# Attention backward: dK and dV by 64-row matmuls with two heads side by side, and a new order of the program

**Chip, cores, metric.** One Trainium2 chip, one core. The metric is the device time of one execution in microseconds (us), the median of several. Ratios and intervals use fast runs alone: the mean time of one kernel's fast runs over that of the other's of the same rounds, so a ratio is not quite that of the medians that are quoted. The span of a profile is some 1.8 us shorter than the time of the same execution (735.8 and 737.6 us before).

**Names.** PE multiplies matrices and writes to the memory PSUM; DVE and ACT copy from there and do the vector work; POOL does small work and the small DMA transfers; SP issues the large transfers.

## The reference

Forward and backward of grouped-query attention, all in bf16: 32 batches, 4 key heads, 32 query heads with 4 queries each (so 32 query rows per key head, 128 in all), 2048 keys, 128 dimensions.

```python
def _fwd_reference(q, k, v):
    ...                                   # k, v repeated 8 times over the heads
    scores = jnp.einsum("bhqd,bhkd->bhqk", q, k) * scale
    p = _softmax(scores, axis=-1)
    return jnp.einsum("bhqk,bhkd->bhqd", p, v)

def reference(q, k, v, grad_out):
    _out, _vjp = jax.vjp(_f, q, k, v)
    _grads = _vjp(grad_out)
    return (_out, *_grads)                # out, dq, dk, dv
```

K, V, dK and dV are 67 MB each and everything else is small, so some 275 MB pass through DMA in any case.

## The kernel before

The program is fully unrolled. Each piece of work ("unit") of a batch has a place in one global order; each engine executes its units in that order. The places, and for every copy out of PSUM whether DVE or ACT does it, stand in long tables that came out of a search. Units of neighbouring batches are interleaved. A batch has these on PE: transposes of K and V (`KT`, `VT`, 16 units of 8 matmuls), transposes `ET`, `DT` (two units each), and scores `S`, `DP`, outputs `O`, `DQ`, and `DV`, `DK` (four units each, of 512 keys). In the cuts below, comments and `...` are mine.

```python
BLOCK, TRIG, FIRST, FETCH, BACK = 256, 216, 446, 3.4, 0.33    # planner: PE's program blocks
...                                                            # tables PLACE, ENGINE, SHIFT, SWAP
        elif name == "dop":
            t["dop"] = sm_pool.tile([P, D], BF16, name="dop_sb")
            nc.gpsimd.tensor_scalar(out=t["dop"][:], in0=t["go"][:], scalar1=t["rinv"][:], scalar2=None, op0=ALU.mult)
...
        elif name in ("DV", "DK"):
            ...
            lhs, rhs = ("e", "dop") if name == "DV" else ("ds", "qp")
            for j in range(CPQ):                      # 4 blocks of 128 keys
                c = CPQ * i + j
                for h in range(NH):                   # 4 heads, one row tile of 32 each
                    r = slice(32 * h, 32 * h + 32)
                    w = QW * (h % 2) + P * j
                    nc.tensor.matmul(accs[h // 2][:, w:w + P], lhsT=t[lhs][r, P * c:P * c + P],
                                     rhs=t[rhs][r, :], start=True, stop=True, tile_position=(32 * h, 0))
...
        elif name in ("Os", "DQs"):                   # stores of O and dQ, on POOL's queue
            nc.gpsimd.dma_start(...)
...
    with tc.manual_schedule():
        for u in order:
            emit(u)
```

A matmul is two PE instructions, a weight load and the matmul itself (14,400 of each on the page of this kernel). A batch has 900 PE instructions.

## Time and profile before

| | before |
|---|---|
| time, median of 4 | 736.72 us (734.19 to 740.49) |
| PE busy, instructions | 613.7 us, 28,800 |
| DVE, ACT busy | 581.7 us each |
| DMA | 274.74 MB, mean 373 GB/s |
| mean granted PE clock | 0.982 |

Matmuls overlap in PE's pipeline (in this trace a narrow one takes 214 ns in the median, and 16 of them follow each other in 0.33 us), so "busy" is the time in which at least one is in it. A wait marked "issue" has no releaser in the profile: no semaphore, no other engine. The lines themselves are in the prediction.

### The profile page before, as it was taken

How to read it: one execution, taken by the hardware profiler on the slowest of the kernel's cores; microseconds unless marked ns; L12 is line 12 of the kernel's file. 1: busy time of each engine (PE TensorE's matmuls, PEld its weight loads, DVE VectorE, ACT ScalarE, POOL GpSimd, SP SyncE). 2: the span in 40 equal slices, each digit the busy share in tenths (PEclk: the TensorE clock that was granted, in tenths of full speed). 3: DMA queues.
4: the chain of work that ended last, by engine and by line, in shares of the span. 5: the costliest groups of instructions: out<-in, count | busy, mean ns of one | idle time of the engine just before them, and what ended most of it. 6: DMA issues, size and time to landing. Idle time of an engine off the chain costs nothing.

```text
span 735.8 us, 32599 instructions
## 1 busy us (share of the span) xinstructions
PE 613.7 (83%) x14400; PEld 458.3 (62%) x14400; DVE 581.7 (79%) x835; ACT 581.7 (79%) x862; POOL 112.0 (15%) x230
## 2 busy tenths in 40 slices
PE   6798887988878988888888898887988878898885
PEld 5576665665655765656666666665766656676563
DVE  3788887878877887877878788887878878888874
ACT  4788886878877887877877688886888878887884
POOL 3121110111101111111111111110111111110110
PEclk9999999999999999999999999999999999999998
DMA  9999999999999999999999989999999999989957
GB/s 346 408 401 407 378 411 355 392 383 346 401 356 390 370 400 365 390 400 342 389 355 395 396 331 402 377 402 404 348 402 366 401 383 386 372 314 389 378 222 283
DMA packets 75917, 274.74 MB, mean 373 GB/s; under 512 B 8192, under 2 KB 8192, under 8 KB 75776
## 3 DMA queue, kind: packets, MB, share of 16 engines
q1 hardware_dynamic: 71680, 268.46, 94.7%
q0 software_dynamic: 4096, 4.20, 1.7%
q8 instruction: 112, 1.84, 0.9%
q14 instruction: 29, 0.24, 0.1%
HBM read 136.31 MB, written 136.31 MB: 371 GB/s over the span
## 4 chain that ended last, share of the span: by engine, by line
PE 66%; issue 10%; ACT 9%; DMA 8%; DVE 6%; SPq 0%; DVEq 0%; POOLq 0%; ACTq 0%; POOL 0%
PE psum L426 31%; PE psum L488 10%; PE psum L525 9%; PE psum L437 9%; PE psum L477 7%; ACT dk_sb L530 4%; DMA v_sb<-in_v_dram 4%; DVE ds_sb L510 4%; DMA k_sb<-in_k_dram 3%; ACT dt_sb L394 2%; ACT e_sb L453 2%; DMA out_dram<-dv_sb 1%; DVE dv_sb L530 1%; DVE mjunk L444 1%; ACT vt_sb L394 1%
## 5 line engine op out<-in xcount | busy, mean ns | idle before, releaser
L426 PE MATMUL psum<-ident,v_sb 128*128 128x128 bf16 x2048 | 159.9, 222 | 38.3 <-DVE ds_sb L510 13.1
L426 PEld LDWEIGHTS <-v_sb 128*128 128x128 bf16 x2048 | 122.5, 99 | 89.5 <-issue 68.0
L530 ACT CAST dv_sb<-psum 128x1024 bf16<-128x1024 f32 x158 | 155.8, 1025 | 12.4 <-PE psum L525 9.0
L530 ACT CAST dk_sb<-psum 128x1024 bf16<-128x1024 f32 x161 | 157.8, 1025 | 9.6 <-PE psum L525 9.3
L426 PE MATMUL psum<-ident,k_sb 128*128 128x128 bf16 x2048 | 149.5, 222 | 6.7 <-DMA k_sb<-in_k_dram 4.6
L530 DVE CAST dk_sb<-psum 128x1024 bf16<-128x1024 f32 x95 | 113.6, 1221 | 32.1 <-PE psum L525 29.0
L426 PEld LDWEIGHTS <-k_sb 128*128 128x128 bf16 x2048 | 119.5, 99 | 26.5 <-issue 8.9
L530 DVE CAST dv_sb<-psum 128x1024 bf16<-128x1024 f32 x98 | 119.4, 1220 | 17.9 <-PE psum L525 17.7
L397 DVE COPY vt_sb<-psum 128x1024 bf16<-128x1024 bf16 x128 | 87.3, 684 | 36.5 <-PE psum L426 25.7
L394 ACT COPY vt_sb<-psum 128x512 f32<-128x512 f32 x128 | 77.8, 610 | 40.4 <-PE psum L426 40.2
L397 DVE COPY kt_sb<-psum 128x1024 bf16<-128x1024 bf16 x126 | 84.2, 683 | 19.9 <-PE psum L426 17.3
L394 ACT COPY kt_sb<-psum 128x512 f32<-128x512 f32 x130 | 74.7, 615 | 22.9 <-PE psum L426 22.0
L525 PE MATMUL psum<-qp_sb,ds_sb 32*128 32x128 bf16 x2048 | 62.0, 218 | 29.3 <-ACT et_sb L394 9.4
L510 DVE SCALAR_TENSOR_TENSOR ds_sb<-psum,delta,e_sb 128x1024 bf16<-128x1024 f32 x64 | 81.8, 1278 | 1.0 <-PE psum L437 1.0
L453 ACT ACTIVATE e_sb<-psum,m 128x1024 bf16<-128x1024 f32 x64 | 70.8, 1112 | 6.3 <-DVE mjunk L444 4.7
L525 PEld LDWEIGHTS <-ds_sb 32*128 32x128 bf16 x2048 | 34.6, 93 | 49.8 <-issue 36.1
L525 PE MATMUL psum<-dop_sb,e_sb 32*128 32x128 bf16 x2048 | 60.5, 217 | 4.9 <-issue 2.2
L488 PE MATMUL psum<-k_sb,dt_sb 128*32 128x128 bf16 x2048 | 49.1, 224 | 12.5 <-issue 12.3
L499 POOL DMA_DIRECT2D out_dram<-dq_sb x32 | 17.8, 557 | 265.4 <-ACT dq_sb L495 250.5
L477 PE MATMUL psum<-ident,e_sb 128*128 128x128 bf16 x512 | 38.8, 219 | 16.2 <-ACT dk_sb L530 14.1
L462 POOL TENSOR_SCALAR dop_sb<-go_sb,rinv 128x128 bf16<-128x128 bf16 x32 | 19.7, 616 | 211.8 <-DVE rinv L459 209.3
L525 PEld LDWEIGHTS <-e_sb 32*128 32x128 bf16 x2048 | 35.8, 92 | 22.9 <-issue 8.8
(44 smaller groups left out, 643.2 us busy)
## 6 DMA issues: line engine op xcount, KB each, us to landing
k_sb<-in_k_dram SPq DMA_DIRECT2D x128, 512.0 KB, 8.9
v_sb<-in_v_dram SPq DMA_DIRECT2D x128, 512.0 KB, 8.8
out_dram<-dv_sb SPq DMA_DIRECT2D x64, 1024.0 KB, 8.0
out_dram<-dk_sb SPq DMA_DIRECT2D x64, 1024.0 KB, 7.7
q_sb<-in_q_dram POOLq DMA_DIRECT2D x32, 32.0 KB, 5.4
go_sb<-in_grad_out_dram POOLq DMA_DIRECT2D x32, 32.0 KB, 5.7
out_dram<-o_sb POOLq DMA_DIRECT2D x32, 32.0 KB, 5.1
out_dram<-dq_sb POOLq DMA_DIRECT2D x32, 32.0 KB, 6.1
```

Source lines behind the costliest of these rows:

```text
L394: nc.scalar.copy(out=out.rearrange("p c d -> p (c d)").bitcast(FP32), in_=in_.rearrange("p c d -> p (c d)").bitcast(FP32))
L397: nc.vector.tensor_copy(out=out, in_=in_)
L426: nc.tensor.transpose(out=ps[:, j, :], in_=t[x, h][:, 8 * i + j, :], identity=ident[:])
L437: nc.tensor.matmul(t[name, i][r, QW * w:QW * w + QW], lhsT=t["qdt"][:, side, r], rhs=t[x, h, i][:, CPQ * w:CPQ * w + CPQ, :], start=True, ...
L453: nc.scalar.activation(out=t["e"][:, 2 * QW * i:2 * QW * i + 2 * QW], in_=t["S", i][:], func=ACT.Exp, bias=t["m"][:], scale=scale, accum_o ...
L462: nc.gpsimd.tensor_scalar(out=t["dop"][:], in0=t["go"][:], scalar1=t["rinv"][:], scalar2=None, op0=ALU.mult)
L477: nc.tensor.transpose(out=ps[:, j, :], in_=src[:, P * c:P * c + P], identity=ident[:])
L488: nc.tensor.matmul(t[name][r, 0:D], lhsT=t[xt, c // 8][:, c % 8, r], rhs=t[x, h][:, c, :], start=(c == 0), stop=(c == C - 1), tile_positio ...
L499: nc.gpsimd.dma_start(out=(o_r if name == "Os" else dq_r)[b], in_=t["o" if name == "Os" else "dq"][:])
L510: nc.vector.scalar_tensor_tensor(out=t["ds"][:, w], in0=t["DP", i][:], scalar=t["dl"][:], in1=t["e"][:, w], op0=ALU.subtract, op1=ALU.mult)
L525: nc.tensor.matmul(accs[h // 2][:, w:w + P], lhsT=t[lhs][r, P * c:P * c + P], rhs=t[rhs][r, :], start=True, stop=True, tile_position=(32 * ...
L530: copy(out=t[name[:2], "out", g][:, :, CPQ * i:CPQ * i + CPQ, :].rearrange("p h c d -> p h (c d)"), in_=t[name[:2], i][g][:].rearrange("p ...
```

## The change

Intent: fewer PE instructions, so that PE waits less for its own program. Two heads share one matmul of 64 rows; the moving operand has 256 columns, of which one half is zero in the rows of each head, so the heads' results come out side by side. POOL makes the two masked halves. Along with it all tables were made anew, with the wide form's costs in the planner, the planner's model of block fetches was changed, and stores of O and dQ moved to some four batches later.

```diff
-BLOCK, TRIG, FIRST, FETCH, BACK = 256, 216, 446, 3.4, 0.33
+BLOCK, TRIG, FIRST, FETCH, BACK = 256, 216, 446, 3.15, 0.33
...                                        (PLACE, SHIFT, SWAP: all numbers new)
-    QTe="D", KTe="DADADAAD", VTe="ADDADAAD", ETe="AA", DTe="AA", Oe="D", DQe="A", DVe="AADAADAD", DKe="ADAAADAD")
+    QTe="A", KTe="DADAAAAA", VTe="ADDADAAD", ETe="AA", DTe="AD", Oe="D", DQe="A", DVe="AADAADAD", DKe="DAAAADAD")
...
+            if b == 2:
+                nc.gpsimd.memset(evenodd[:], 0.0)
...                                        (1 or scale where row's head is even / odd)
-            t["dop"] = sm_pool.tile([P, D], BF16, name="dop_sb")
-            nc.gpsimd.tensor_scalar(out=t["dop"][:], in0=t["go"][:], scalar1=t["rinv"][:], scalar2=None, op0=ALU.mult)
+            t["dop"] = dop_bd[b % CAP["dop"]]
+            for k in range(2):
+                nc.gpsimd.tensor_scalar(out=t["dop"][:, k, :], in0=t["go"][:], scalar1=t["rinv"][:],
+                                        scalar2=evenodd[:, k:k + 1], op0=ALU.mult, op1=ALU.mult)
...                                        (qp the same)
-                for h in range(NH):
-                    r = slice(32 * h, 32 * h + 32)
-                    w = QW * (h % 2) + P * j
-                    nc.tensor.matmul(accs[h // 2][:, w:w + P], lhsT=t[lhs][r, P * c:P * c + P],
-                                     rhs=t[rhs][r, :], start=True, stop=True, tile_position=(32 * h, 0))
+                for g in range(2):
+                    r = slice(64 * g, 64 * g + 64)
+                    nc.tensor.matmul(accs[g][:, 2 * P * j:2 * P * j + 2 * P], lhsT=t[lhs][r, P * c:P * c + P],
+                                     rhs=t[rhs][r, :, :].rearrange("p h d -> p (h d)"), start=True, stop=True,
+                                     tile_position=(64 * g, 0))
...                                        (the copies out of PSUM read the new layout)
```

## The prediction

> **What bounds the kernel now.** I read the busy row first, then the slices, the queues and the chain, then single batches. The page says that no compute engine is full, and that the DMA engines nearly are:
>
> ```profile
> PE 613.7 (83%) x14400; PEld 458.3 (62%) x14400; DVE 581.7 (79%) x835; ACT 581.7 (79%) x862; POOL 112.0 (15%) x230
> ...
> DMA  9999999999999999999999989999999999989957
> ...
> q8 instruction: 112, 1.84, 0.9%
> ...
> PE 66%; issue 10%; ACT 9%; DMA 8%; DVE 6%; SPq 0%; DVEq 0%; POOLq 0%; ACTq 0%; POOL 0%
> ```
>
> The row of DMA digits tempts one to stop: the engines are busy, so the change can win nothing. But the kernel moves 274.74 MB at a mean of 373 GB/s, and single stretches reach over 400, so some of the time is lost. The chain is mostly PE, with 10% "issue": time in which an engine waited for nothing that the profile shows. The q8 line says what this may be: 112 packets of 16 KB, that is one per 256 of the 28,800 PE instructions. PE's program itself comes in by DMA.
>
> I then cut the middle into batches (the 32 reciprocals on DVE mark them) and asked for busy time, granted clock and GB/s of each:
>
> ```profile
> 398.80:423.20 24.40, 20.24 (x454) 14.82 (x453) 18.17 (x27) 18.28 (x27) 3.48 (x7) 0.93 1.02 400
> 423.20:444.10 20.90, 18.47 (x452) 14.04 (x450) 18.01 (x26) 18.16 (x27) 3.48 (x7) 1.00 0.91 339
> 444.10:467.00 22.90, 18.74 (x453) 14.12 (x450) 18.02 (x26) 18.28 (x27) 3.48 (x7) 1.00 1.02 404
> 467.00:488.00 21.00, 18.57 (x453) 13.96 (x450) 18.02 (x26) 18.16 (x27) 3.48 (x7) 1.00 0.99 375
> 488.00:512.20 24.20, 20.23 (x457) 14.96 (x458) 18.16 (x27) 18.27 (x27) 3.48 (x7) 0.93 1.03 406
> 512.20:533.30 21.10, 18.83 (x463) 14.18 (x466) 17.97 (x26) 18.06 (x27) 3.48 (x7) 1.00 0.96 356
> ```
>
> After the span come PE, weight loads, DVE, ACT, POOL, clock, DMA share, GB/s. The same work takes about 21 us in every second batch and 23 to 24.4 in the others. The long ones have the clock at 0.93; the lack of data shows in the batch after (339, 356 GB/s), since a late batch makes its stores late. The PE timeline of a long one shows the cause:
>
> ```profile
> 412.90 0.34 PE L525 MATMUL psum<-qp_sb,ds_sb 32*128 32x128 bf16 x9
> 415.22 0.40 PE L525 MATMUL psum<-qp_sb,ds_sb 32*128 32x128 bf16 x7 [1.98 <-issue]
> 415.55 1.03 PE L426 MATMUL psum<-ident,v_sb 128*128 128x128 bf16 x8
> ```
>
> PE stops inside a group of 16 matmuls that has all its inputs, for 1.98 us, and the transposes after it take 1.03 us in place of 0.62. I numbered PE's instructions in the order of the trace: of all gaps over 0.3 us, 42.9 us stand before one single position of 256 (number 193 modulo 256), no other has over 7.6. At several of those gaps the 16 KB packet lands just as PE resumes. So these are waits for the program. A long batch loses 1.98 us standing and about 1.7 us at half clock (0.07 x 24.4), which is the 3.5 us by which it is longer. My reading: DMA supply and PE limit together, and what spoils PE's part is instruction fetch.
>
> [...] the trace has eight transposes 0.55 us apart, 8 x 56 ns and some 0.1 us for the mode change. [...] the trace has 0.93 in batches with a long stop and 1.00 in the others. [...] 16 matmuls of 128 columns follow each other in 0.33 us, that is 4 x 56 ns plus 0.1.
>
> **The change, part by part.** (1) dV and dK are made with 64-row tiles: two heads share a matmul, and its 256 moving columns hold the rows of one head beside those of the other, with zeros where they don't belong. Per 512-key group that is 8 matmuls of 256 columns in place of 16 of 128, two at once in place of four. *Cost:* 4 x 109 + 110 = 545 ns a group in place of 334 (the timeline's spacing), so 0.21 us more; there are 8 groups in a batch and 256 in all: 54 us of PE time. Summing the spacings of all groups, PE needs 566 us before (17.7 a batch) and 620 after (19.4).
>
> (2) *Gain:* PE instructions fall from 900 to 772 a batch, 28,800 to 24,704, so 96 blocks in place of 112. More than the number counts where they lie. [...] In the old order a run dV, O, O, O, O, dV is 192 instructions in about 2 us[...]. So nearly all of the 42 us should go, and with it the half clock behind the long stops. Also 772 is 3 x 256 + 4: the boundaries fall at nearly the same places in each batch. I leave 5 us of stops.
>
> (3) POOL makes two masked copies of dO' and Q' in place of one each: 64 more operations of 0.37 to 0.62 us (the rows of its two), about 30 us on an engine that is 15% busy. In front of the first dV of a batch this adds up to 0.6 us.
>
> (4) The order is new: stores of O and dQ are issued some four batches later, so POOL no longer blocks on them; about two K copies a batch go from DVE to ACT and one dS-transposed copy the other way. With 613 ns on ACT and 684 on DVE each this is around +20 us ACT and -25 DVE, both still near 80%. PSUM copies read in pieces of 128 rather than 512 elements; I count no cost for that.
>
> *Sum.* The first reciprocal starts at 17.5 us, the last at 711.8, 31 periods of 22.4 on average, and 24 us follow. Without fetch stops a period is what the undisturbed batches show, 20.9 to 21.1. That cannot hold for all: 8.59 MB a batch at the 400 to 409 GB/s of full stretches is 21.2 us. I add 0.3 us because PE now fills 19.4 of it and has less room for its other waits: 21.5. The tail is bound by PE and copies, so it gets 8 x 0.21 = 1.7 us longer. 17.5 + 31 x 21.5 + 25.7 = 709.7; I say 709.
>
> **The rivals.** *PE becomes the bound.* The undisturbed batches have 21.0 - 17.7 = 3.3 us of other PE waits. If all of these are needed, a period is 19.4 + 3.3 = 22.7, and the time 747. For it: PE at 66% of the chain. Against: in those batches PE also waits for loads, and the DMA queue has its own limit of 21.2, so part of the 3.3 us is slack. Half of it real gives 21.2 anyway. *The transfers hide it all.* If the DMA rate of 373 GB/s is the memory's own and the stops only move waiting about, the time stays at 725 to 737. For it: nines everywhere. Against: 339 and 356 GB/s beside 404 in neighbouring batches. *POOL in the way.* If the second masked copy delays each dV, 31 x 0.6 = 19 us come back: 728. Against: POOL sat idle 209 us waiting for the reciprocal, and other PE work stands between softmax and the first dV in the order.
>
> **Range and chances.** The DMA floor is 274.74 MB at 405 GB/s, 678 us, plus some 3 us at the head and 16 at the tail where little moves: 697, which is why I go no lower than 698. A period of 22.0 (half the rivals' losses) gives 725, the upper end at 727. "Faster by over 2%" starts at 722, a mean period of 21.9. I give that 0.75, within 2% 0.23 (mostly rival one and three), slower 0.02.
>
> **What would show it.** Right: PE busy up by 30 to 60 us and 12,352 matmuls; q8 with about 96 packets; "issue" waits of PE down by 40 us or more; the granted clock near 1.00 in the middle; batches of even length at 21.2 to 21.8 us; GB/s near 400 in most slices. Wrong: batches even but at 22.5 with PE waiting for ACT or DVE (rival one); fetch stops still there, at a new fixed place of each batch; waits of PE for the masked copies (rival three); the dV and dK groups at other than 0.55 us.

## The result, and the profile after

708.88 us (707.75 to 711.37, 10 runs) against 736.34 (16 runs); ratio 0.9624, 95% interval 0.960 to 0.9647: faster by 3.8%.

In all that follows, a "stop" is the time from the start of one PE instruction to that of the next, where it is over 0.3 us and stands before position 193 modulo 256. It includes what the earlier instruction still runs: of the 42.9 us before, some 34 are idle time, of the 6.1 us after some 4.4.

The page of the changed kernel, in the same rows as in the prediction, with two rows of the costliest groups added:

```profile
PE 634.1 (90%) x12352; PEld 471.4 (67%) x12352; DVE 559.6 (79%) x779; ACT 606.4 (86%) x918; POOL 134.1 (19%) x303
...
DMA  8999999999999999999999999999999999999967
...
q8 instruction: 96, 1.57, 0.8%
...
PE 52%; DMA 25%; ACT 10%; DVE 7%; issue 4%; POOL 0%; DVEq 0%; POOLq 0%; ACTq 0%
...
L472 POOL TENSOR_SCALAR dop_sb<-go_sb,rinv,evenodd 128x128 bf16<-128x128 bf16 x64 | 27.9, 439 | 532.7 <-DVE rinv L468 507.7
...
L536 PE MATMUL psum<-dop_sb,e_sb 64*128 64x256 bf16 x1024 | 87.1, 271 | 1.9 <-DVE et_sb L400 0.5
```

"issue" fell from 10% to 4% of the chain, and DMA rose from 8% to 25%: the end is now set by transfers to a good part. The stops are 6.1 us, against 42.9. The granted clock in the middle was at half for 20.5 us before (six windows of 3.4 us) and for 3.4 us after.

The batches, cut at the reciprocals as before (columns: span, PE, weight loads, DVE, ACT, POOL, clock, DMA share, GB/s):

```profile
295.10:315.80 20.70, 19.45 (x390) 14.60 (x388) 17.25 (x25) 18.99 (x30) 4.16 (x9) 1.00 1.03 411
336.50:357.20 20.70, 19.45 (x391) 14.59 (x388) 17.25 (x25) 19.00 (x30) 4.16 (x9) 1.00 1.02 408
...
485.90:507.60 21.70, 19.56 (x390) 14.64 (x388) 17.36 (x25) 19.18 (x30) 4.16 (x9) 1.00 1.02 400
507.60:529.30 21.70, 19.55 (x392) 14.64 (x389) 17.38 (x25) 19.17 (x30) 4.16 (x9) 1.00 1.01 393
```

The alternation of 21 and 24 us is gone. In its place there are two flat stretches: every batch from 233 to 399 us takes 20.7 us, and those from there to 573 us take 21.6 (two of them 22.4). PE's busy time is the same in both. The PE timeline of a late batch has the difference, one wait for a load:

```profile
516.59 0.61 PE L536 MATMUL psum<-dop_sb,e_sb 64*128 64x256 bf16 x8
518.11 1.51 PE L435 MATMUL psum<-ident,k_sb 128*128 128x128 bf16 x24 [0.91 <-DMA k_sb<-in_k_dram]
```

And the time from issue to landing (last column) of K loads grows over the run. Loads issued in 100 to 150 us, then in 500 to 550 us:

```profile
k_sb<-in_k_dram SPq DMA_DIRECT2D x11, 512.0 KB, 8.3
...
k_sb<-in_k_dram SPq DMA_DIRECT2D x10, 512.0 KB, 14.9
```

My reading, tested below: the engines now take data faster than DMA can bring it. K loaded ahead hides this for half of the run; then the batches go at the DMA's pace.

### The profile page after: what moved, and what is told of

It reads as the page before. It is cut to its first block, busy times and chain, and to the rows that moved or that the text cites.

```text
span 706.3 us, 28517 instructions
## 1 busy us (share of the span) xinstructions
PE 634.1 (90%) x12352; PEld 471.4 (67%) x12352; DVE 559.6 (79%) x779; ACT 606.4 (86%) x918; POOL 134.1 (19%) x303
## 4 chain that ended last, share of the span: by engine, by line
PE 52%; DMA 25%; ACT 10%; DVE 7%; issue 4%; POOL 0%; DVEq 0%; POOLq 0%; ACTq 0%
DMA k_sb<-in_k_dram 24%; PE psum L435 22%; PE psum L536 12%; PE psum L500 8%; PE psum L489 5%; DVE mjunk L453 5%; PE psum L446 4%; ACT dk_sb L542 3%; ACT e_sb L462 3%; ACT dv_sb L542 2%; DMA go_sb<-in_grad_out_dram 1%; DVE vt_sb L400 1%; ACT qdt_sb L397 1%; DVE ds_sb L522 1%; PE psum L424 0%
## 5 line engine op out<-in xcount | busy, mean ns | idle before, releaser
L435 PE MATMUL psum<-ident,v_sb 128*128 128x128 bf16 x2048 | 148.9, 220 | 1.2 <-ACT dk_sb L542 0.6
L397 ACT COPY kt_sb<-psum 128x512 f32<-128x512 f32 x185 | 106.9, 604 | 27.4 <-PE psum L435 26.3
L472 POOL TENSOR_SCALAR dop_sb<-go_sb,rinv,evenodd 128x128 bf16<-128x128 bf16 x64 | 27.9, 439 | 532.7 <-DVE rinv L468 507.7
L400 DVE COPY vt_sb<-psum 128x1024 bf16<-128x1024 bf16 x132 | 88.1, 686 | 35.8 <-PE psum L435 35.7
L536 PE MATMUL psum<-qp_sb,ds_sb 64*128 64x256 bf16 x1024 | 86.3, 270 | 5.2 <-DVE ds_sb L522 0.7
L536 PE MATMUL psum<-dop_sb,e_sb 64*128 64x256 bf16 x1024 | 87.1, 271 | 1.9 <-DVE et_sb L400 0.5
L397 ACT COPY vt_sb<-psum 128x512 f32<-128x512 f32 x124 | 70.5, 590 | 15.5 <-PE psum L435 15.1
L536 PEld LDWEIGHTS <-ds_sb 64*128 64x128 bf16 x1024 | 50.1, 93 | 27.2 <-issue 11.6
L400 DVE COPY kt_sb<-psum 128x1024 bf16<-128x1024 bf16 x71 | 48.4, 684 | 22.4 <-PE psum L435 22.1
L536 PEld LDWEIGHTS <-e_sb 64*128 64x128 bf16 x1024 | 43.5, 94 | 23.9 <-issue 7.7
L500 PEld LDWEIGHTS <-dt_sb 128*32 128x32 bf16 x2048 | 33.0, 96 | 24.1 <-issue 11.4
L453 DVE TENSOR_SCALAR_CACHE_REDUCE mjunk<-psum,m 128x1024 bf16<-128x1024 f32 x32 | 41.1, 1284 | 8.0 <-DVE mjunk L453 3.3
```

What stands on the lines that cost most here:

```text
L397: nc.scalar.copy(out=out.rearrange("p c d -> p (c d)").bitcast(FP32), in_=in_.rearrange("p c d -> p (c d)").bitcast(FP32))
L400: nc.vector.tensor_copy(out=out, in_=in_)
L435: nc.tensor.transpose(out=ps[:, j, :], in_=t[x, h][:, 8 * i + j, :], identity=ident[:])
L453: nc.vector.tensor_scalar(out=junk[:], in0=t["S", i][:], scalar1=-scale, scalar2=t["m"][:] if i else None, op0=ALU.mult, op1=ALU.min, accu ...
L472: nc.gpsimd.tensor_scalar(out=t["dop"][:, k, :], in0=t["go"][:], scalar1=t["rinv"][:], scalar2=evenodd[:, k:k + 1], op0=ALU.mult, op1=ALU. ...
L500: nc.tensor.matmul(t[name][r, 0:D], lhsT=t[xt, c // 8][:, c % 8, r], rhs=t[x, h][:, c, :], start=(c == 0), stop=(c == C - 1), tile_positio ...
```

## The experiments

My theory was that fewer PE instructions remove the fetch stops and that this is the gain. The rival: the new order is the gain. In the edits, "wide" is the new form, "narrow" the old one.

### Form and order apart

The first run takes the kernel before and changes only the form (POOL's masked copies, matmuls, layout of the copies out of PSUM, as in the diff above); tables and planner stay.

> The kernel before with its own order and bank plan, only dV and dK made as in the change (64-row tiles, 256 columns, masked copies on POOL, 24,704 PE instructions). Theory 1 (instruction fetch): the stops of PE at position 193 modulo 256 fall from about 42 us to under 10, PE busy rises by 20 to 55 us, and the time is 708 to 722 us although the order was not laid out for it. Rival (the new order does it: late O and dQ stores, copies moved between DVE and ACT): the form alone only costs 54 us of PE time, so 737 us or more.

The second takes the changed kernel and puts the narrow form back, reading the right half of the masked operand (and the old layout in the copies out of PSUM):

```diff
-                for g in range(2):                    # 64 rows, 256 columns
-                    ...
+                for h in range(NH):
+                    r = slice(32 * h, 32 * h + 32)
+                    w = QW * (h % 2) + P * j
+                    nc.tensor.matmul(accs[h // 2][:, w:w + P], lhsT=t[lhs][r, P * c:P * c + P],
+                                     rhs=t[rhs][r, h % 2, :], ..., tile_position=(32 * h, 0))
```

> The changed kernel with its new order, POOL work and engine split, but dV and dK again as 16 matmuls of 32 rows and 128 columns a group (28,800 PE instructions). Theory 1: stops of some 40 us and half clock behind them return, 728 to 742 us, although PE has 54 us less to do. Rival (the order does it): 705 to 711 us, no slower than the change, as PE has less work.

The third and fourth keep PE's columns of the wide form and bring back the number of instructions, in the new and in the old order:

```diff
-                for g in range(2):
-                    ... accs[g][:, 2*P*j : 2*P*j + 2*P], rhs=t[rhs][r, :, :]
+                for k in range(2):
+                    for g in range(2):
+                        r = slice(64 * g, 64 * g + 64)
+                        w = 2 * P * j + P * k
+                        nc.tensor.matmul(accs[g][:, w:w + P], ..., rhs=t[rhs][r, k, :], ...)
```

> The changed kernel with each 64-row matmul of 256 columns split into two of 128 with the same weights: the same columns through PE, the same POOL, PSUM and order, but 28,800 instructions again. This is the instruction count by itself. Theory 1: [...] so some 20 us of stops and 718 to 732 us. Rival: 707 to 712 us, as nothing but the number of instructions changes.

> The old order with the split form: PE time of the change (54 us more than before) without fewer instructions. Theory 1: half the stops of before plus 54 us more PE time, 730 to 748 us, clearly slower than the old order with 256 columns. Rival (order): as the old order with 256 columns, within 1%.

Measured, medians in us, and in brackets the stops in the profiled run (for split that is the slowest of four in the new order, 732.5 us, and the fastest in the old one, 750.6):

| | narrow, 28,800 instructions | split, 28,800 | wide, 24,704 |
|---|---|---|---|
| old order | 737.2 (42.9: the kernel before) | 755.9 (26.5) | 731.4 (7.7) |
| new order | 723.0 (67.4) | 725.1 (42.2) | 708.9 (6.1: the change) |

(The change is from its own rounds. Split costs PE some 12 ns a group over wide, 8 x 56 against 4 x 109, 3 us in all by this estimate; the median of single groups is 553 ns against 543 or 544.) Ratios to the kernel before of the same rounds: old wide 0.9929 (0.9896 to 0.9961), old split 1.023 (1.0173 to 1.0288), new narrow 0.979 (0.9736 to 0.9844), new split 0.9845 (0.9776 to 0.9915).

Several of my ranges were missed: old wide by both theories (708 to 722, and 737 or more), new narrow by both (728 to 742, and 705 to 711), old split above (730 to 748). New split fell into its range (718 to 732), but with 42 us of stops where I expected 20.

What follows. *The number of instructions matters by itself:* from split to wide, with the same columns through PE, 24.5 us go in the old order and 16.2 in the new, and the stops with them. *PE time matters too, in the old order:* from narrow to split 18.7 us come on top there, although the stops fall by 16; in the new order 2.1 us come on top while the stops fall by 25, so there the two can't be told apart. *The order matters at least as much as the form:* it takes off 14.2 us in narrow, 30.8 in split, 22.5 in wide; the form takes off 5.8 in the old order and 14.1 in the new. The two don't add up: 5.8 + 14.2 is 20 of the 28 us, and the rest comes only with both; the new order's tables were made with the wide form's costs. So neither theory holds alone. Nor does the sum of the stops tell the time: narrow in the new order has 24.5 us more of them than the kernel before and is 14.2 us faster.

Why the form alone brought so little, the batches of the wide form in the old order show:

```profile
507.70:529.70 22.00, 19.98 (x389) 14.38 (x386) 18.11 (x27) 18.36 (x27) 4.20 (x9) 1.00 1.01 391
529.70:551.60 21.90, 19.88 (x388) 14.38 (x386) 18.02 (x26) 18.36 (x27) 4.21 (x9) 1.00 1.00 389
```

They are even, so the stops are gone here (7.7 us are left in the whole run), but each takes 22 us at 390 GB/s, and K loads land 9 us after issue all along. From this I take it that the loop of the engines is the limit and not the DMA; this kernel was not run with fewer bytes. Its PE waits, from the PE timeline of one batch:

```profile
530.51 0.86 PE L537 MATMUL psum<-qp_sb,ds_sb 64*128 64x256 bf16 x8 [0.19 <-ACT et_sb L398]
531.91 0.61 PE L490 MATMUL psum<-ident,e_sb 128*128 128x128 bf16 x8 [0.54 <-ACT dk_sb L543]
...
548.89 0.61 PE L436 MATMUL psum<-ident,v_sb 128*128 128x128 bf16 x8 [0.56 <-ACT vt_sb L398]
550.23 0.61 PE L436 MATMUL psum<-ident,v_sb 128*128 128x128 bf16 x8 [0.73 <-DVE ds_sb L523]
```

Together 2.02 us. The new order at the same place of the loop has three:

```profile
317.37 0.61 PE L489 MATMUL psum<-ident,e_sb 128*128 128x128 bf16 x8 [0.32 <-ACT dk_sb L542]
...
332.90 0.61 PE L446 MATMUL psum<-vt_sb,qdt_sb 128*32 128x512 bf16 x8 [0.23 <-ACT vt_sb L397]
...
335.13 0.22 PE L424 MATMUL psum<-ident,q_sb 128*128 128x128 bf16 x1 [0.62 <-ACT e_sb L462]
```

That is 1.17 us, so 0.85 less. And PE's busy time is 19.45 in place of some 19.9 us with the same matmuls: in the new order units of like tiling stand next to each other (22 changes of mode a batch in place of 27, counted in the two programs; at 0.1 us a change, measured below, that is 0.5 us), and 0.85 + 0.5 is about the 1.3 us from 22.0 to 20.69.

### Two limits

Theory A: after the change the loop needs 20.69 us and DMA more, which appears when the loads fetched ahead are used up. Both kernels were run with half of each dV store left out, 12% fewer bytes. Their outputs are wrong, which doesn't matter for the times.

```diff
-            nc.sync.dma_start(out=(dv_r if name == "DVs" else dk_r)[b, g],
-                                in_=t[name[:2], "out", g][:].rearrange("p h c d -> p h (c d)"))
+            n = 1 if name == "DVs" else 2
+            nc.sync.dma_start(out=(dv_r if name == "DVs" else dk_r)[b, g][:, :n, :],
+                              in_=t[name[:2], "out", g][:, :n].rearrange("p h c d -> p h (c d)"))
```

> The changed kernel, storing only one of two heads of each dV tile (64 stores of 0.5 MB in place of 1 MB, 12% fewer bytes; dV is wrong on purpose). In the changed kernel the batches take 20.69 us up to some 375 us and 21.65 us after that, with loads landing later and later. Theory A (two limits: the fixed loop of the engines takes 20.69 us, the DMA needs 21.65, and loads fetched ahead hide this at first): all middle batches at 20.6 to 20.8 us, landing times level, 684 to 694 us. Rival B (the second half is long because block boundaries drift 4 instructions a batch into bad places): the 21.65 us batches stay, 702 us or more.

> The kernel before with the same 12% fewer bytes (dV wrong on purpose). Theory A (before is held by PE and its fetch stops, DMA has room): little to win, 720 to 737 us, with stops of PE still at position 193 modulo 256. Rival (before is held by the DMA rate, as its row of nines suggests): 12% of the DMA time goes, 670 to 700 us.

The changed kernel fell to 694.87 us, ratio 0.9432 (0.9381 to 0.9483), just above the range of 684 to 694. From the 7th to the 29th period all but one take 20.7 to 20.8 us (that one 21.0), the second half like the first, and K loads issued in 100 to 200 and in 450 to 550 us land after nearly the same time:

```profile
k_sb<-in_k_dram SPq DMA_DIRECT2D x20, 512.0 KB, 6.4
...
k_sb<-in_k_dram SPq DMA_DIRECT2D x20, 512.0 KB, 7.5
```

So 20.69 is the loop of the engines, and the transfers make 21.6 of it in this kernel; the drift of block boundaries (rival B) is out. What SP waits for says the same. From 400 to 572 us in the changed kernel it waits 115.9 us for landings (the first two lines are the largest), with fewer bytes none:

```profile
SPq L546 <- DMA out_dram<-dv_sb: 39.0, 16, 2.6
SPq L421 <- DMA out_dram<-dk_sb: 28.1, 15, 2.6
```

The kernel before went to 730.39 only, ratio 0.9887 (0.9845 to 0.9928), with 34.5 us of stops still there. In spite of its row of nines, DMA was not its main limit.

### What in the rest of the change counts

POOL: the masked copies of dO' made twice (`for k in (0, 1, 0, 1)` in place of `range(2)`).

> The changed kernel with the two masked copies of dO' made twice on POOL (64 more operations of 0.44 us, so the first dV of a batch has its operand about 0.9 us later; the result is the same). If the masked copies are on the path (the third rival of the prediction): 31 x 0.9 = up to 27 us more, 720 to 737 us. If they have room: within 0.5% of the change.

710.6 us, ratio 0.964 (0.959 to 0.969): nothing. The third rival is out.

The stores of O and dQ back at once behind their copies:

```diff
+            if name in ("Os", "DQs"):
+                x = name[:-1] + "e"
+                u.at = b * PERIOD + 0.3 + PLACE[x][i] + (SHIFT[special][x][i] if special in SHIFT else 0.0)
```

> The changed kernel with the stores of O and dQ put back right behind the copies that they store, as in the order before; all other engines keep the new order. If the late stores are what makes the new order faster (POOL blocked on dQ holds up the masked copies of the next batch): 712 to 725 us. If the order gains on PE itself: within 0.5% of the change.

710.68 us, ratio 0.9643 (0.9591 to 0.9695): nothing. That POOL blocks on these stores (in the kernel before it waited 250.5 us for the dQ copies ahead of them, after the change 15.5) does no harm.

The old division of copies in the middle batches (`QTe="D", KTe="DADADAAD", DTe="AA"`):

> The changed kernel with the old division of copies between DVE and ACT in its middle batches (K copies, Q copy and dS-transposed copies back where they were; 24 of 32 batches or more); order of PE and POOL as in the change. If the new order's gain comes from the division of copies: 715 to 728 us, with new PE waits for DVE. If it comes from PE's own order (fewer mode changes, shorter waits in the loop): within 1% of the change.

707.99 us, ratio 0.9574 (0.9501 to 0.9647). The period is 21.2 us in each from the 11th to the 26th, longer than 20.69, and the total is the same:

```profile
400.00:421.20 21.20, 19.68 (x391) 14.74 (x388) 18.24 (x27) 18.46 (x29) 4.16 (x9) 1.00 1.02 402
421.20:442.40 21.20, 19.68 (x389) 14.76 (x388) 18.23 (x27) 18.46 (x28) 4.17 (x9) 1.00 1.02 405
```

This fits the two limits: what the faster loop wins early it gives back later. But it also shows that 21.6 is no fixed limit of DMA, which here brings a batch in 21.2 us. SP waits for landings for 10.3 us from 400 to 572 us, not for 115.9. Both undone together, so that of the new order only the sequence of units is left (with the bank plan and the tables of the first and last batches that go with it):

> Both earlier undoings at once: the changed kernel with the old division of copies between DVE and ACT in the middle batches and with the early stores of O and dQ. What stays of the new order is the sequence of groups on PE, DVE and ACT and of transfers on the DMA queue. If that sequence is the part of the order that pays: 704 to 714 us, a loop of about 21.2 us as with the old division alone. If each of the two undone parts can stand in for the other: 716 us or more.

706.56 us, ratio 0.9567 (0.9489 to 0.9644). So it is the sequence of units on the engines and of transfers that pays, not the division of copies nor the late stores. Its interval overlaps that of the change (0.960 to 0.9647), so I don't call it better. The sequence could not be split further: putting the old sequence of transfers under the new one of the engines didn't build, as a load then stood after its use. Which of the two sequences pays stays open.

Only dV wide, dK narrow, 26,752 instructions:

> The changed kernel with only dV in the wide form and dK in the old narrow form: 836 PE instructions a batch, 27 us less PE time than the change, 26,752 instructions. [...] If instructions matter more than PE time: 711 to 720 us, between change (709) and narrow form (723). If PE time matters as much: at or below 709, a better kernel than the change.

709.55 us, ratio 0.9618 (0.9566 to 0.967), with 15.4 us of stops: as fast as the change, below my 711 to 720. Some batches take 20.2 us here and some 23, and K loads land after 14 us in the second half as well. I read this as a few stops being hidden where DMA is the limit; that was not tested.

## Why the prediction was right, and where not

*The time* was 709 predicted, 708.9 measured. The agreement is better than its steps, and so partly luck. The sum is also one of spans: 709.7 us of span would be some 711.5 of time.

*The time of a wide group* was right: 545 ns foreseen, 544 the median of 196 single groups in the trace. The 109 ns for 256 columns in it were an estimate; they lie on the line through the 56 ns between matmuls of 128 columns and the 216 ns between the quickest sets of four of 512 columns in the trace before. In the trace after, a wide matmul starts 109 ns after the last but one (median), in the trace before a narrow one 56 ns after the fourth before it: two and four row tiles side by side. Pairs of a weight load and a matmul of 128 columns, in the transposes, follow each other at 56 ns in both. *The summed cost of 54 us was too high:* PE busy rose by 20.4 us only, below the "30 to 60" I had named, and within one order by 31.4 (old) and 35.8 (new, from 598.3). The 334 ns of a narrow group were its best case: before, 86 of 192 single groups took it, and the median was 417 (waits and stops included). The new order's fewer mode changes, which I hadn't counted, are the rest by an estimate of 5 x 0.1 x 32 = 16 us; from the old to the new order PE busy falls by 15.4 us in narrow and 11 in wide. The kernel before also had more half-clock time, in which busy time is stretched: eight transposes took 1.03 us there in place of 0.62.

*The gain from fetch* was right in size and place, as far as the stops go: 42.9 us became 6.1, where I had left 5; 96 blocks; granted clock 1.00 in the middle except for one window of 3.4 us. The step from crowded instructions to "nearly all of the 42 us" was my estimate: when a block is asked for, the traces don't show. The profile's "issue" waits of PE's matmuls fell by 30 us (33.8 to 3.8), not by the 40 I had named. That the stops come from the number of instructions, the split form shows. That they are waits for the program, the packets show, though not as I read them: a packet doesn't land "just as PE resumes". At 36 of the 37 stops before, its transfer had ended 1.2 to 1.6 us earlier, and no boundary was crossed sooner than 1.2 us after it. I had left this time out.

*The half clock* I put too simply. In the six batches shown, the one from 444.1 has a stop of 1.87 us at a clock of 1.00, and of the eight stops of 1.8 us or more in the run, half clock sets in at four.

*The step that fell* is "Without fetch stops a period is what the undisturbed batches show, 20.9 to 21.1", with "the order is new" booked as about neutral. Free of stops, the old order takes 22.0 us, because the added PE time meets waits that are not slack. That is the first rival, for which I had put 22.7 and 747 us; in the old order it came true in part (22.0 and 731), in the new order it didn't, since this order took 1.3 us out of the loop. I had assumed the slack; the order made it. Between half and four fifths of the 28 us (14.2 to 22.5) go with the order, according to which of the two is changed first.

*The DMA floor* was right as a mean: 21.2 us a batch at 405 GB/s. The batches were not even at it, as I had expected: the 20.69 us of the middle beat it for a while on loads fetched ahead, then came 21.6; the mean of 31 periods is 21.35 where I had 21.5. The first reciprocal came at 19.9 in place of 17.5 us, the rest after the last one is 24.5 in place of 25.7: 19.9 + 31 x 21.35 + 24.5 = 706.3, the profiled span.

*The second rival* (transfers hide it all) is refuted for the kernel before by its lightened form; after the change transfers do set the pace of the second half. *ACT* I had near 80%; it is at 86%, which follows from my own +20 us in the shorter span.

## What to carry to other kernels

When PE stops with its inputs ready, number its instructions and see whether the stops share one position modulo 256, as the 42.9 us here shared 193; what helped here was fewer and longer instructions where short ones are crowded, even at more columns (narrow to wide: 5.8 us in the old order, 14.1 in the new). But a stop's length is not the gain: take the stops away with everything else in place, as the wide form in the old order did, and see which loop comes to light. And a row of nines for DMA doesn't tell whether DMA is the limit: under one, 12% fewer bytes took 1.1% off the kernel before. The time from issue to landing tells more, but not alone. It stayed near 9 us where the engines set the pace (before, and wide in the old order), and grew from 8.3 to 14 us and then stayed there where DMA did. With the old division of copies it grew to 13 us too, while the engines kept a flat 21.2. What SP waits for (landings or engines) told these cases apart, and the run with fewer bytes tested it.

## What the traces show of the hardware

- PE's program came in blocks of 16 KB, one per 256 instructions (112 packets for 28,800, 96 for 24,704). The stops at their boundaries were 42.9 us in the 112 blocks before (37 stops, up to 2.2 us each), where 128-column matmuls with 32-row or 32-column tiles crowd; 67.4 us in another order. Half clock came on top (20.5 us in six windows before), behind some of the long stops.
- From the end of a block's transfer to its use it was never under 1.2 us in the traces before and after, and mostly 1.2 to 1.6 where PE stood waiting for it; from the start of the transfer it was never under 2.2 us. Before, the 256 instructions ahead of a stop took 4.77 us in the median (37 stops), those ahead of the other boundaries 6.27; in the changed kernel those ahead of a boundary without a stop took 6.90.
- A group of 16 column-tiled matmuls takes 0.34 us before a group of another mode and 0.23 before one of its own mode (medians of 60 and of 50 in the changed kernel): 0.1 us a change.
- What an overfull DMA queue costs: the changed kernel in its DMA-bound stretch had 21.6 us a batch with loads landing after 14.9 us; with the old division of copies the loop ran at a flat 21.2 us with loads landing after 13.1 us. Why a fuller queue should be slower, if it is that, stays open.
